# A gated mixture of experts after a depthwise convolution: the second part's first eight scatters as a group of their own, and an even two scatters a block

## The chip, the cores and the metric

The kernel runs on one core of a Trainium2 chip. The metric is the device time of one launch in microseconds (us), the median of several runs. A profile of one execution gives the time of each instruction on each engine: PE (matrix products), DVE (vector), ACT (activations and copies), POOL (here mainly the issuer of indirect DMAs) and SP (here the issuer of plain DMAs).

## The reference: what is computed

The input `x` has 8 sequences of 3584 tokens with 192 channels. A causal convolution with 7 softmaxed taps per head gives every token its row. Then each token goes to one of 8 experts: the expert with the highest logit where the token's local gate is below 0.5 (or at the start of a sequence), otherwise the expert of the token before it. The expert is a two-layer network, 192 to 1024 to 192.

```python
for b in range(B):
    prev_e = -1
    for s in range(S):
        fresh_e = int(np.argmax(logits[b, s]))
        if s == 0 or local_gate[b, s] < 0.5:
            e = fresh_e
        else:
            e = prev_e if prev_e >= 0 else fresh_e
        prev_e = e
        ...
        h = np.maximum(x[b, s] @ w1[e], 0.0)
        out[b, s] = p[e] * (h @ w2[e])
```

## The kernel before, in words

All products are in float32. The 28672 tokens are cut into 16 parts of 1792 tokens (`PT`). For each part the kernel does three things: it convolves (`conv`, for parts 0 and 1 a wider form on PE, `wide`), it routes (`route`, or `wide_route`: logits, expert, the token's place among the tokens of its expert), and it scatters the rows into `slots`, a table in DRAM with a stretch for each expert. A scatter (`put`, L762) is one indirect DMA from POOL: in part 0 and part 1 a part has 16 of them with 112 rows each, later 14 with 128 rows each. They wait in the list `to_put`, an entry of which is the group number, the rows and the places.

The expert networks run over **blocks** (L879 to L881): first 35 units of 128 tokens, then blocks of two units, then the rest. A unit is run as soon as it is surely full. `ONE` (L54) gives how many units are surely full after part g whatever the routing: 7 after part 0, 21 after part 1, 35 after part 2. So blocks 0 to 6 belong to group 0, blocks 7 to 20 to group 1, blocks 21 to 34 to group 2. `tables(g)` (L748) calls `table` (L782), 19 small DVE instructions that write the expert and the row of every unit of group g; part 0 has a form of its own, `first_table`.

A block does this, in order, in the loop at L1128:

- `ensure` (L1080) issues the row loads of the blocks up to three ahead on SP (`load_rows`, L901). The first load of a group waits for every scatter of that group to land (L909 to L913). A load is left for a later round if scatters of its group are still in `to_put`.
- `weights` issues the expert's weights of the block three ahead on SP (`load_w`, 1.5 MB, four buffers).
- `hidden` (L941) runs the first layer on PE (L952) and ACT (L957), and after each half issues as many scatters as `shares` says.
- `turn` (L922) transposes the rows of the next block on PE (L356) and copies them on ACT (L938).
- `output` (L962) runs the second layer on PE (L969) into two PSUM buffers `yps`. ACT scales one half into `o_sb` (L977, two buffers), DVE adds the other half (L981), and an indirect DMA from POOL sends the rows to the result (L985).
- `step` fills DVE with instructions of the next convolution and routing, by a budget of time per call; they stand in DVE's queue ahead of L981.

Each engine takes its instructions in the order written out by the program. SP's queue holds rows and weights mixed, so a row load that waits holds back the weights behind it. Indirect DMAs of `put` and of `output` go through one software queue.

In `wide_route` for part 1 (L390), the scatters are listed at L484 and L485, and then `place` and `base` (the tokens so far of every expert) and the tables follow at L489 to L493, all before the loop of blocks begins. The 16 scatters of part 1 are issued in blocks 1 to 4, four a block: `shares` is (1, 3) for blocks 1 to 4.

Of the kernel before, what the change touches and what calls it, by code (L numbers as in the profile page):

```python
# [9 lines left out]
I32 = mybir.dt.int32  # L10
Act = mybir.ActivationFunctionType
Alu = mybir.AluOpType
# [5 lines left out]
P = 128  # L18
# [5 lines left out]
UT = 128  # L24
NT = 14
PT = P * NT
NPART = N // PT
# [5 lines left out]
NH = NB // 2  # L33
# [14 lines left out]
def _sure(tokens, size):  # L48

    return max(0, -(-(tokens - E * (size - 1)) // size))  # L50
# [2 lines left out]

ONE = [_sure(min(g + 1, EARLY) * PT, UT) for g in range(NPART)]  # L54
TWO = [_sure((g + 1) * PT - ONE[-1] * UT, BT) if g >= EARLY else 0 for g in range(NPART)]
REST = NU - ONE[-1] - 2 * TWO[-1]
DG = 3 + D + DR
Y0 = 2
# [19 lines left out]
def kernel(  # L78
# [10 lines left out]
    nc = tc.nc  # L89
    cst = ctx.enter_context(tc.tile_pool(name="cst", bufs=1))  # L90
# [9 lines left out]
    op = ctx.enter_context(tc.tile_pool(name="op", bufs=2))  # L100
# [90 lines left out]
    def wide(g, xv, y_sb, both):  # L191
# [75 lines left out]
        for q in range(4):  # L267
# [8 lines left out]
                            base=0, pattern=[[1, P]], channel_multiplier=-1)  # L276
# [34 lines left out]
    eo = cst.tile([P, E], F32, name="eo")  # L311
# [25 lines left out]
    base = cst.tile([P, E], F32, name="base")  # L337
# [10 lines left out]
    tabi = {}  # L348

    def halves():  # L350
        return [(half, slice(half * DR, (half + 1) * DR)) for half in range(2)]
# [38 lines left out]
    def wide_route(g, y_sb, lt):  # L390

        y, tr = y_sb[:TB], ident[:TB, :TB]
# [63 lines left out]
        if g:  # L456
# [4 lines left out]
                                                op=Alu.is_equal)  # L461
# [9 lines left out]
        upto = sm.tile([P, E, 1 + NB], F32, name="upto")  # L471
# [9 lines left out]
        posi = sm.tile([P, NB], I32, name="posi", bufs=3)[:TB]  # L481
        nc.vector.tensor_copy(posi, pos)
        nc.vector.tensor_tensor(y[:, :, 0], pr, rs, op=Alu.mult)
        for b in range(NB):  # L484
            to_put.append((g, y[:, b, :], posi[:, b:b + 1]))  # L485
        yield
        if g == 0:
            first_table(upto[:, :, NB], pos)
        nc.vector.tensor_copy(place, upto[:, :, NB])  # L489
        nc.vector.tensor_tensor(base, place, eo, op=Alu.subtract)  # L490
        if g:
# [256 lines left out]
    def tables(g):  # L748
        if ONE[g] > (ONE[g - 1] if g else 0):
            yield from table(0, g, 1, ONE[g])  # L750
        if TWO[g] > (TWO[g - 1] if g else 0):
            yield from table(1, g, 2, TWO[g])
        if g == NPART - 1:
# [3 lines left out]
    to_put = []  # L757
    puts = []
# [23 lines left out]
    def table(kind, g, size, cap):  # L782


        end = ends[kind]
        new = sm.tile([P, E], F32, name="new")
        ni = sm.tile([P, E], I32, name="ni")
        nc.vector.scalar_tensor_tensor(new, used, -float(UT), base, Alu.mult, Alu.add)
        yield 0.2
        if cap is None:  # L790
            nc.vector.tensor_scalar(new, new, float(UT - 1), None, Alu.add)
            yield 0.2
        nc.vector.tensor_copy(ni, new)
        yield 0.2
        nc.vector.tensor_scalar(ni, ni, (UT * size).bit_length() - 1, None, Alu.arith_shift_right)
        yield 0.2
        nc.vector.tensor_copy(new, ni)
        yield 0.2
        nc.vector.tensor_copy(end[:, 0:1], end[:, E:])
        yield 0.2  # L800
        nc.vector.tensor_tensor_scan(end[:, 1:], new, new, end[:, 0:1], Alu.add, Alu.max)
        yield 0.2
        if cap is not None:
            nc.vector.tensor_scalar(end, end, float(cap), None, Alu.min)
            yield 0.2
        inn = sm.tile([P, E], F32, name="inn")
        nc.vector.tensor_scalar(inn, end[:, :E], i_of, None, Alu.is_le)
        yield 0.2
        nc.vector.scalar_tensor_tensor(inn, end[:, 1:], i_of, inn, Alu.is_gt, Alu.mult)
        yield 0.2  # L810

        row = sm.tile([P, E], F32, name="row")
        nc.vector.scalar_tensor_tensor(row, end[:, :E], -float(size), used, Alu.mult, Alu.add)
        yield 0.2
        nc.vector.tensor_tensor(row, row, eb, op=Alu.add)
        yield 0.2
        add = sm.tile([P, 3, E], F32, name="add")
        nc.vector.scalar_tensor_tensor(add[:, 0, :], row, pf[:, size - 1:size], inn,
                                       Alu.add, Alu.mult)
        yield 0.2  # L820
        nc.vector.tensor_tensor(add[:, 1, :], ef, inn, op=Alu.mult)
        yield 0.2
        nc.vector.tensor_copy(add[:, 2, :], inn)
        yield 0.2
        sums = sm.tile([P, 3], F32, name="sums")
        nc.vector.tensor_reduce(sums, add, axis=AX.X, op=Alu.add)
        yield 0.2
        nc.vector.tensor_tensor(tab[kind], tab[kind], sums, op=Alu.add)
        yield 0.2
        ti = cst.tile([P, 2], I32, name=f"tabi{kind}_{g}")  # L830
        if cap is None:

            no = sm.tile([P, 1], F32, name="no")
            nc.vector.tensor_scalar(no, tab[kind][:, 2:3], -float(DUMMY), float(DUMMY),
                                    Alu.mult, Alu.add)
            yield 0.2
            nc.vector.tensor_tensor(tab[kind][:, 0:1], tab[kind][:, 0:1], no, op=Alu.add)
            yield 0.2
        nc.vector.tensor_copy(ti, tab[kind][:, 0:2])
        yield 0.2  # L840
        tabi[kind, g] = ti
        nc.vector.tensor_tensor(new, end[:, 1:], end[:, :E], op=Alu.subtract)
        yield 0.2
        nc.vector.scalar_tensor_tensor(used, new, float(size), used, Alu.mult, Alu.add)
        yield 0.2
# [30 lines left out]
            to_put.append((g, pad, toi[:, e:e + 1]))  # L876


    blocks = [(0, 1, i, next(g for g in range(NPART) if i < ONE[g])) for i in range(ONE[-1])]  # L879
    blocks += [(1, 2, i, next(g for g in range(NPART) if i < TWO[g])) for i in range(TWO[-1])]  # L880
    blocks += [(2, 1, i, NPART - 1) for i in range(REST)]  # L881

# [18 lines left out]
    def load_rows(i):  # L901
        n, group = blocks[i][1], blocks[i][3]
        r = entry(i, 0, DUMMY + 1 - n)
        xg = xp.tile([P, KT, DG], F32, name="xg")
        get = nc.sync.dma_start(
            out=xg[:, :n, :].rearrange("p k d -> p (k d)"),
            in_=slots.rearrange("(r p) d -> r (p d)", p=UT)[bass.ds(r, n)]
            .rearrange("o (p x) -> (o p) x", x=n * DG))
        if group not in waited:  # L909
            waited.add(group)  # L910
            for g, ins in puts:
                if g == group:
                    tc.add_manual_dep(get.ins, ins.name, SYNC, reason="a row of the block")  # L913
        for g in range(group + 1, NPART):
            if any(p[0] == g for p in puts):
                tc.declare_no_dep(get.ins, group=f"puts{g}", reason="not in a unit full before")
        tc.add_to_no_dep_group("gets", get.ins)
        return xg
# [22 lines left out]
    def hidden(n, wb, xT, shares=(1, 1)):  # L941
        hT = hp.tile([P, FK, BT], F32, name="hT")
        w = slice(0, n * P)


        for two in range(2):
            hps = [hps_p.tile([P, 2, BT], F32, name="hps") for half in range(2)]
            for d in range(KD):
                for j in range(2):
                    f0 = (d * 4 + two * 2 + j) * P  # L950
                    for half, rows in halves():
                        nc.tensor.matmul(hps[half][:, j, w], lhsT=wb[rows, f0:f0 + P],  # L952
                                         rhs=xT[rows, d, w], start=(d == 0 and j == 0),
                                         stop=(d == KD - 1), skip_group_check=True)
            for half in range(2):
                m = half * 4 + two * 2
                relu = nc.scalar.activation(hT[:, m:m + 2, w], hps[half][:, :, w], Act.Relu)  # L957
            for _ in range(shares[two]):
                put(relu)
        return hT  # L960
# [117 lines left out]
    wbs, xgs = {}, {}  # L1078
# [40 lines left out]
    xT, _ = turn(blocks[0][1], xgs[0])  # L1119
# [8 lines left out]
    for i, (_, n, _, _) in enumerate(blocks):  # L1128
        st["block"] = i
        ensure(i)  # L1130
        weights(i + AHEAD)
        if i == LATE:
            x_in[3] = load_x(3)

        hT = hidden(n, wbs[i], xT, (0, 0) if i == 0 else (1, 3) if i < 5 else (1, 1))
        if i + 1 < len(blocks):
            xT, copied = turn(blocks[i + 1][1], xgs[i + 1])
            if len(to_put) > NT // 2 and n == KT:
                put(copied)
        step(2.1 if n == 1 else 4.2)  # L1140
        output(n, wbs.pop(i), xgs.pop(i), hT)
        step(1.3 if n == 1 else 3.0)

    kind, _, at, group = spare[0]
    any_left = nc.values_load(tabi[kind, group][at:at + 1, 0:1], min_val=0, max_val=DUMMY,  # L1145
                              skip_runtime_bounds_check_because="an entry of the table")
    with tc.If(any_left < DUMMY):
        for block in spare:
            blocks.append(block)
            i = len(blocks) - 1  # L1150
            n = block[1]
            xg = load_rows(i)
            wb = load_w(i)
            xT, _ = turn(n, xg)
# [68 lines left out]
```

## Time and profile before

| | |
|---|---|
| median of 3 runs | 1362.19 us (1357.04 to 1363.54) |
| span of the profiled execution | 1335.1 us |
| PE busy | 1314.4 us, 98% |
| DVE, ACT, POOL busy | 58%, 38%, 37% |
| DMA mean over the span | 255 GB/s |

The profiled execution is shorter than the timed ones, so times within the launch are read from the profile, and the forecast takes differences from it and puts them on the median. The profile's table of slices has PE at 98 or 99 per cent nearly everywhere but in the first four slices of 33 us, and the granted PE clock at full speed but for the third, which has 0.8 of it. The change lies in that stretch: blocks 0 to 20 run from about 45 us to 170 us. A timeline line has start, duration, engine and line, operation, tiles, count, and in brackets how long the engine was idle before it and for what.

### The profile page before, as it was taken

Reading aid. Unit: us, or ns where it says so; the run is one execution under the profiler, and the core shown is the slowest. Engines: PE = TensorE matmul, PEld = TensorE weight load, DVE = VectorE, ACT = ScalarE, POOL = GpSimd, SP = SyncE. Lnnn points to the kernel's source line nnn. Section 1 sums busy time; section 2 is a strip of 40 time slices with the busy share of each in tenths; the row PEclk is TensorE's granted clock in tenths of the full one; section 3 lists DMA queues with packets and bytes.
Section 4 is the critical chain, followed back from the end, with each engine's and each line's share of the span. In section 5 each row is a group of like instructions: output and inputs, shape, how many; then the busy total and the mean of one; then the engine's idle time right before and its main releaser. Section 6 shows DMA issues by size and latency. Waiting matters only on the chain. (4 is left out here: it accounts for less than half of the span.)

```text
span 1335.1 us, 41872 instructions
## 1 busy us (share of the span) xinstructions
PE 1314.4 (98%) x17140; PEld 1256.5 (94%) x17140; DVE 775.9 (58%) x2414; ACT 510.6 (38%) x1147; POOL 493.3 (37%) x538
## 2 busy tenths in 40 slices
PE   8889999999999999999999999999999999999998
PEld 7889999999999999999999999999999999999997
DVE  5969898977878787878787878785600000000000
ACT  5334444434343434343434343433333333333333
POOL 4544353534343434343434343434343211111111
PEclk9989999999999999999999999999999999999999
DMA  4899999966676767676767676756566555556993
GB/s 187 303 359 397 393 379 360 405 252 252 222 262 211 273 211 273 225 259 222 263 222 262 223 261 225 260 208 217 209 224 213 197 189 193 197 186 235 319 325 123
DMA packets 67299, 340.39 MB, mean 255 GB/s; under 512 B 12576, under 2 KB 23191, under 8 KB 47650
## 3 DMA queue, kind: packets, MB, share of 16 engines
q1 hardware_dynamic: 44784, 284.88, 59.0%
q0 software_dynamic: 22320, 52.82, 10.4%
q8 instruction: 136, 2.23, 0.6%
q14 instruction: 57, 0.47, 0.1%
q10 hardware_dynamic: 2, 0.00, 0.0%
HBM read 284.73 MB, written 53.41 MB: 253 GB/s over the span
## 5 line engine op out<-in xcount | busy, mean ns | idle before, releaser
L969 PE MATMUL yps<-wb,hT 64*128 64x192 f32 x7328 | 632.0, 325 | 0.2 <-issue 0.2
L952 PE MATMUL hps<-xT,wb 64*128 64x256 f32 (+1 forms) x6816 | 626.2, 336 | 4.7 <-ACT ls L579 3.0
L952 PEld LDWEIGHTS hps<-xT,wb 64*128 64x128 f32 x6816 | 563.4, 187 | 44.6 <-ACT ls L579 3.2
L969 PEld LDWEIGHTS yps<-wb,hT 64*128 64x128 f32 x7328 | 597.7, 188 | 2.8 <-issue 2.7
L985 POOL DMA_INDIRECT out_dram<-o_sb,xg x229 | 231.8, 1012 | 644.1 <-DVE o_sb L981 574.8
L957 ACT ACTIVATE hT<-hps 128x512 f32<-128x512 f32 (+1 forms) x568 | 261.3, 512 | 351.7 <-PE hps L952 351.7
L384 DVE SCALAR_TENSOR_TENSOR y_sb<-x_sb,c,y_sb 128x336 f32<-128x336 f32 x672 | 377.3, 571 | 18.1
L981 DVE SCALAR_TENSOR_TENSOR o_sb<-yps,xg,o_sb 128x192 f32<-128x192 f32 x229 | 87.4, 413 | 484.6 <-ACT o_sb L977 482.7
L769 POOL DMA_INDIRECT slots<-y_sb,posi x228 | 229.1, 1005 | 169.6 <-ACT hT L957 93.0
L977 ACT ACTIVATE o_sb<-yps,xg 128x192 f32<-128x192 f32 x229 | 86.9, 418 | 431.0 <-PE yps L969 417.7
L938 ACT COPY xT<-xps 128x768 f32<-128x768 f32 (+1 forms) x142 | 96.8, 682 | 7.3 <-PE xps L356 7.3
L356 PEld LDWEIGHTS xps<-ident,xg 64*128 64x128 f32 x1374 | 67.3, 139 | 11.8 <-DMA xg<-slots 2.4
L356 PE MATMUL xps<-ident,xg 64*128 64x64 f32 x1374 | 68.7, 222 | 3.5 <-DMA xg<-slots 3.5
L374 ACT ACTIVATE y_sb<-x_sb,c 128x336 f32<-128x336 f32 x112 | 64.6, 589 | 0.0
L564 DVE STREAM_TRANSPOSE z<-y_sb 128x768 f32<-128x768 f32 (+1 forms) x56 | 45.4, 853 | 0.4
L590 DVE COPY lt<-lq 32x36 f32<-32x36 f32 x224 | 40.9, 183 | 3.5
L574 PE MATMUL hps<-z,wg 64*32 64x128 f32 x1344 | 24.5, 273 | 1.3 <-issue 1.3
L574 PEld LDWEIGHTS hps<-z,wg 64*32 64x32 f32 x1344 | 20.0, 105 | 3.5 <-issue 2.0
L560 POOL COPY y_sb<-y_sb 128x896 f32<-128x896 f32 x14 | 13.3, 952 | 0.0
L548 PE MATMUL yps<-y_sb 112*128 112x194 f32 x64 | 11.5, 331 | 1.8 <-DVE y_sb L542 1.8
L548 PEld LDWEIGHTS yps<-y_sb 112*128 112x128 f32 x64 | 10.4, 189 | 2.6 <-DVE y_sb L542 2.0
L666 DVE COPY bk<-so_far 1x32 f32<-1x32 f32 x56 | 12.3, 220 | 0.7
(238 smaller groups left out, 366.9 us busy)
## 6 DMA issues: line engine op xcount, KB each, us to landing
wb<-in_w_dram SPq DMA_DIRECT2D x138, 1536.0 KB
x_sb<-in_x_dram SPq DMA_DIRECT2D x14, 1920.0 KB
xg<-slots SPq DMA_DIRECT2D x87, 259.0 KB
xg<-slots SPq DMA_DIRECT2D x53, 129.5 KB
wb<-in_w_dram SPq DMA_DIRECT2D x12, 512.0 KB
out_dram<-o_sb,xg POOLq DMA_INDIRECT x229
slots<-y_sb,posi POOLq DMA_INDIRECT x228
x_sb<-in_xb_dram SPq DMA_DIRECT2D x4, 768.0 KB
```

The lines of the kernel that those rows point to most:

```text
L356: nc.tensor.transpose(to, src[rows], identity=ident[rows, rows])
L374: nc.scalar.activation(cols(h), chans(h, 0), Act.Copy, scale=c[:, h, 0:1])
L384: nc.vector.scalar_tensor_tensor(cols(h), chans(h, k), c[:, h, k:k + 1], cols(h), Alu.mult, Alu.add)
L564: nc.vector.transpose(z[:, t:u, :], y_sb[:, t:u, Y0:Y0 + D])
L769: ins = nc.gpsimd.indirect_dma_start(out=slots[:, :], in_=rows, in_offset=None, out_offset=bass.IndirectOffsetOnAxis(ap=to, axis=0)).ins
L938: copied = nc.scalar.copy(to, at)
L952: nc.tensor.matmul(hps[half][:, j, w], lhsT=wb[rows, f0:f0 + P], rhs=xT[rows, d, w], start=(d == 0 and j == 0), stop=(d == KD - 1), skip_g ...
L957: relu = nc.scalar.activation(hT[:, m:m + 2, w], hps[half][:, :, w], Act.Relu)
L969: nc.tensor.matmul(yps[half][:, k * D:(k + 1) * D], lhsT=hT[rows, m, k * P:(k + 1) * P], rhs=wb[rows, WA + m * D:WA + (m + 1) * D], start= ...
L977: nc.scalar.activation(o_sb[:, k, :], y[k][0], Act.Copy, scale=xg[:, k, 0:1])
L981: nc.vector.scalar_tensor_tensor(o_sb[:, k, :], y[k][1], xg[:, k, 0:1], o_sb[:, k, :], Alu.mult, Alu.add)
L985: sent = nc.gpsimd.indirect_dma_start(out=out, in_=o_sb[:, k, :], in_offset=None, out_offset=bass.IndirectOffsetOnAxis(ap=xg.bitcast(I32)[ ...
```

## The change

Part 1 is split in two groups for scattering and for tables. `HALF` is 0.5, a group number between 0 and 1. `FULL` says how many units are surely full after each group: 7 after group 0, 14 after `HALF` (2688 tokens), 21 after group 1, and so on. The first eight scatters of part 1 (its first 896 tokens) carry the group `HALF`, and a table is written for this group, from the counts after eight of the sixteen chunks. Blocks 7 to 13 now belong to `HALF`, so their first row load waits for eight scatters and not for sixteen. Further, `shares` is (1, 1) from block 1 on: part 1 is scattered in blocks 1 to 8, two a block. The purpose is that block 7's rows no longer wait for all of part 1, and that scatters do not crowd in four blocks.

```diff
+HALF = 0.5
+FULL = {0: ONE[0], HALF: _sure(PT + PT // 2, UT), **{g: ONE[g] for g in range(1, NPART)}}
...
         for b in range(NB):
-            to_put.append((g, y[:, b, :], posi[:, b:b + 1]))
+            to_put.append((HALF if g and b < NH else g, y[:, b, :], posi[:, b:b + 1]))
         yield
         if g == 0:
             first_table(upto[:, :, NB], pos)
+        else:
+            nc.vector.tensor_tensor(base, upto[:, :, NH], eo, op=Alu.subtract)
+            for _ in table(0, HALF, 1, FULL[HALF]):
+                pass
...
-        ti = cst.tile([P, 2], I32, name=f"tabi{kind}_{g}")
+        ti = cst.tile([P, 2], I32, name=f"tabi{kind}_{int(2 * g)}")
...
-    blocks = [(0, 1, i, next(g for g in range(NPART) if i < ONE[g])) for i in range(ONE[-1])]
+    blocks = [(0, 1, i, next(g for g in FULL if i < FULL[g])) for i in range(ONE[-1])]
...
-        for g in range(group + 1, NPART):
-            if any(p[0] == g for p in puts):
+        for g in FULL:
+            if g > group and any(p[0] == g for p in puts):
                 tc.declare_no_dep(get.ins, group=f"puts{g}", reason="not in a unit full before")
...
-
-        hT = hidden(n, wbs[i], xT, (0, 0) if i == 0 else (1, 3) if i < 5 else (1, 1))
+        hT = hidden(n, wbs[i], xT, (1, 1) if i else (0, 0))
```

## The prediction

> **What bounds the kernel now.** I read the page first. PE is busy in almost all of the span:
>
> ```profile
> PE 1314.4 (98%) x17140; PEld 1256.5 (94%) x17140; DVE 775.9 (58%) x2414; ACT 510.6 (38%) x1147; POOL 493.3 (37%) x538
> ```
>
> So the change, which takes no work from PE, can only win back time in which PE stands still or runs at a lower clock. The view of waits of PE, from 0 to 300 us, says for what it stood still longest:
>
> ```profile
> PE xps L356 <- DMA xg<-slots: 3.5, 2, 2.1
> PE hps L952 <- ACT ls L579: 3.0, 1, 3.0
> ```
>
> Two waits for rows (3.5 us) and one for ACT (3.0 us). The timeline from 74 to 150 us shows where the larger ones lie, around blocks 6 and 7:
>
> ```profile
> 87.71 0.42 ACT L977 ACTIVATE o_sb<-yps,xg 128x192 f32<-128x192 f32 x1 [7.52 <-DMA out_dram<-o_sb,xg]
> ...
> 88.33 2.25 PE L952 MATMUL hps<-xT,wb 64*128 64x128 f32 x24 [3.00 <-ACT ls L579]
> ...
> 90.58 1.23 SPq L905 DMA_DIRECT2D xg<-slots  x2
> ...
> 92.68 0.58 PE L356 MATMUL xps<-ident,xg 64*128 64x64 f32 x6 [2.10 <-DMA xg<-slots]
> ...
> 93.06 4.41 PE L969 MATMUL yps<-wb,hT 64*128 64x192 f32 x32
> ...
> 97.31 2.84 PE L952 MATMUL hps<-xT,wb 64*128 64x128 f32 x48
> ```
>
> ACT stands 7.52 us in front of an `o_sb` buffer that an output scatter has not yet left; the copy that PE needs is behind it. Then SP issues block 7's rows at 90.58, when the last of the 16 scatters (issued at 82.17) has landed, and PE waits for these rows. After that the second layer takes 4.41 us, where it takes 2.82 at 100.17: the clock is down. The view of windows of 1 us (columns: length, busy PE, weight loads, DVE, ACT, POOL, clock, DMA share, GB/s):
>
> ```profile
> 89.00:90.00 1.00, 1.00 (x18) 1.00 (x16) 0.95 (x5) 0.01 (x1) 0.84 (x1) 0.73 0.18 60
> 90.00:91.00 1.00, 0.58 (x5) 0.29 (x2) 0.92 (x7) 0.70 (x2) 0.00 (x0) 0.50 0.29 98
> ...
> 96.00:97.00 1.00, 1.00 (x14) 1.00 (x14) 0.00 (x0) 0.00 (x0) 0.00 (x0) 0.86 0.99 397
> ```
>
> Half clock from about 89.5 to 96.3, 6.8 us. Price of this stall from block starts (first L952 of each): block 6 to 7 is 97.31 - 83.72 = 13.59 us, and an undisturbed block is 102.82 - 97.31 = 5.51, so 8.08 lost. Block 5 to 6, which also has logits, takes 83.72 - 75.96 = 7.76; the same pair of works later takes 148.56 - 141.43 = 7.13, so 0.63 lost. Together **8.7 us**.
>
> The last view is the timeline of 40 to 75 us, because the change puts DVE work there:
>
> ```profile
> 49.20 0.17 DVE L788 SCALAR_TENSOR_TENSOR new<-used,base 128x8 f32<-128x8 f32 x1
> ...
> 52.67 0.17 DVE L844 SCALAR_TENSOR_TENSOR used<-new,used 128x8 f32<-128x8 f32 x1
> 52.75 3.46 DVE L384 SCALAR_TENSOR_TENSOR y_sb<-x_sb,c,y_sb 128x336 f32<-128x336 f32 x6
> ...
> 56.13 0.41 DVE L981 SCALAR_TENSOR_TENSOR o_sb<-yps,xg,o_sb 128x192 f32<-128x192 f32 x1
> ...
> 56.55 0.40 PE L356 MATMUL xps<-ident,xg 64*128 64x64 f32 x6 [1.45 <-DMA xg<-slots]
> ...
> 56.76 2.85 PE L969 MATMUL yps<-wb,hT 64*128 64x192 f32 x32
> ```
>
> DVE has no gap here: part 1's table, six convolution steps, then block 0's L981, which ends at 56.54. Block 1's second layer starts at 56.76. It writes the PSUM buffer that L981 reads. That PE waited for rows at this moment hides that it could not have gone on much earlier for DVE either.
>
> [...] PE's clock is halved [...] 0.50 for 6.8 us, [...] after a gap of 3.0 us; a gap of 1.45 us (55.1 to 56.55) left it at 1.00. [...] ACT's ready copy at L579 sat behind L977. [...] part 0's last scatter ended on POOL at 52.50 and its waiter went at 54.34, 1.8 us. Under load the trace shows far more (below), so I take the trace. [...]
>
> **The change part by part.**
>
> *Two scatters a block.* POOL's work is the same (16 scatters near 1.0 us), off the path. What matters is the software queue. Before, five indirect DMAs a block (four scatters, one output) in 5.5 us, with DMA share near 1.0. Landings seen by their waiters: the output scatter issued at 70.35 frees `o_sb` for ACT at 78.30, the next (77.12) at 87.71. Five landings in 9.4 us, 1.9 us each: five a block need 9.4 us of a 5.5 us block, so the queue grows. After, three a block need 5.6: nearly balanced. The nearest row for three a block is this kernel's part 2, scattered two a block from 111 us on: its output scatters land about 6 to 7 us after POOL is done with them (104.43 + 0.97 to SP's next row load at 111.90; 110.19 + 0.97 to 118.25), with DMA share 1.0 and no PE or ACT wait. `o_sb` allows about 8.3 us (two blocks, 11.0, less 2.7 from L977 to the scatter's end). So the ACT stall goes, margin about 1.5 us.
>
> *Rows of blocks 7 to 13 wait for eight scatters.* The eighth is issued in block 4. With the PE times of the sum below (block 4 starts near 76) POOL is done with it near 81, landed by 83 to 88; block 7's rows are wanted near 91, and a load takes 2.1 us (90.58 to 92.68). It fits, with 1 to 6 us to spare. SP waits from about 77 to then and holds back weights of block 8, due near 99; before they were issued at 92.38 for 102.82, 10.4 us, without a wait. The second eight end in block 8, and block 14 is far. So the 8.7 us go whole. Part 2's scatters start in block 9 in both.
>
> *One more table.* One subtraction and 19 instructions on DVE. Part 1's table took 49.20 to 52.75 = 3.55 us, the subtraction 0.2: **3.75 us**. A second instance of the table (110.10 to 113.81) gives 3.71, so 3.7 to 3.9. Queued behind it: six convolution steps, L981 of block 0, then its output scatter on POOL and part 1's first scatters. Waiting for L981: PE. L981 ends at 60.3 and not 56.54, block 1's second layer starts near 60.45 and not 56.76: **3.7 us** lost. Nothing gives it back: PE does 5.51 us a block and DVE nine steps and L981, 5.5 us.
>
> *Clock.* PE then idles from 55.1 to 60.45 but for 0.4 us of transposes. [...] I take **1.6**.
>
> *Group numbers, names, no-dependence declarations.* No instruction: nothing.
>
> Sum: -8.7 + 3.7 + 1.6 = **-3.4 us**, 1362.19 - 3.4 = 1358.8.
>
> **The rivals.** *A: no new stall*, DVE's delay being absorbed, because PE waits at 56.55 for rows anyway. For it: PE's named wait there is rows. Against: L981 ended only 0.2 us before. Time 1362.2 - 8.7 = 1353.5. *B: the old stall stays and the new one is added*: the queue is near balance at three a block, and x's load of part 3 falls in this stretch; a late eighth scatter would hold SP again. Then +5.3 with none of the 8.7 won: 1367.5, slower. Against: part 2's stretch ran with three a block. *C: timed runs lose more here than the profile.* They are 25 us longer than the profiled one, and nothing in it says where. If the DMA-saturated first stage is slower in them, the scatter stall is larger too; at twice 8.7, less 5.3, the time is 1350.1. Against: 25 us may be a constant around the launch.
>
> **How the numbers follow.** Forecast 0.50, A 0.20, C 0.15, B 0.15. Within 0.5% means 1355.4 to 1369.0. Medians of three scatter by some 3 us (1357.04 to 1363.54). Faster: most of A (0.15), nearly all of C (0.14), a tail of the forecast (0.08): 0.37. Slower: a good half of B (0.08) and tails (0.03): 0.11. Same: 0.52. Range 1350 to 1367.5, from C's time to B's.
>
> **What would show it.** Right: block 6 to 7 in about 5.5 us, no ACT wait for the output scatter, block 7's rows issued before 88; and PE idle until about 60.4 before block 1's second layer, with L981 of block 0 ending at 60.3, and clock below 1 soon after. Wrong: L981 early or PE not waiting for it (A); SP's row load of block 7 after 90, ACT's wait at L977 still there (B).

## The result and the profile after

| | before | after | ratio (95% interval) |
|---|---|---|---|
| time of the launch, us | 1360.84 (1357.04 to 1363.54, 4 runs) | 1351.43 (1349.61 to 1353.02, 4 runs) | 0.9932 (0.9904 to 0.9961) |

The change takes 9.4 us, 0.68%. The forecast was 3.4 us and, as the likeliest class, "within 0.5%" (0.52, against 0.37 for faster). The median so missed that class, and the interval of the gain reaches from 0.39% to 0.96%. The measured time lies in the range, but near its lower end, at rival C's value; that it lies there is luck, since the range goes so far down only for C, and what C describes did not come (below).

One thing has to be known to read any number below: each series of runs shows the kernel before either at about 1336 us or at about 1357 to 1361 us; the result above and the first three series of experiments are at the **long level**, while the profile of before that the prediction was drawn from (1335.1 us) and the last series are at the **short level**.

So the profile after is to be read against two profiles of before: the one of the prediction (short level) and one of the same kernel at the long level (`r1_before` below). The page of after, busy times of the engines:

```profile
PE 1327.7 (98%) x17140; PEld 1298.5 (96%) x17140; DVE 780.0 (58%) x2434; ACT 512.1 (38%) x1147; POOL 492.6 (36%) x538
```

DVE has the 20 instructions more that the new table costs (2434 against 2414) and 4.1 us more work. The engines' own work is otherwise the same. PE is "busy" for 13 us more than in the shorter profile of before, with the same 17140 matmuls: it is not the amount of work that differs between the levels.

The waits of PE from 44 to 110 us in after:

```profile
PE yps L977 <- ACT hT L965: 4.2, 4, 2.9
PE hps L960 <- issue: 0.4, 2, 0.3
```

The wait for block 7's rows (2.1 us) and the wait for ACT's copy of the logits (3.0 us) are gone, as forecast; so is the other wait for rows, block 1's 1.4 us, which was to stay. The wait for DVE's L989 (L981 before), which the forecast put in their place, is not there. What PE waits for is ACT's L965, the relu of the first layer; each half of the first layer ends in a pair of relus on ACT, and the second layer begins with what the pairs have made. The timeline of after from 54 to 72 us shows why:

```profile
55.00 0.66 ACT L965 ACTIVATE hT<-hps 128x256 f32<-128x256 f32 x2 [4.92 <-remote]
...
55.43 2.93 PE L977 MATMUL yps<-wb,hT 64*128 64x192 f32 x16 [2.91 <-ACT hT L965]
...
58.15 4.52 PE L960 MATMUL hps<-xT,wb 64*128 64x128 f32 x48
...
61.14 0.41 DVE L989 SCALAR_TENSOR_TENSOR o_sb<-yps,xg,o_sb 128x192 f32<-128x192 f32 x1
...
62.69 2.82 PE L977 MATMUL yps<-wb,hT 64*128 64x192 f32 x32
...
68.59 0.27 PE L960 MATMUL hps<-xT,wb 64*128 64x128 f32 x1
...
68.89 0.95 POOL L777 DMA_INDIRECT slots<-y_sb,posi  x1 [0.30 <-issue]
...
70.36 0.66 ACT L965 ACTIVATE hT<-hps 128x256 f32<-128x256 f32 x2 [2.26 <-PE xps L360]
70.79 1.28 PEld L977 LDWEIGHTS yps<-wb,hT 64*128 64x128 f32 x16 [0.69 <-ACT hT L965]
```

Two things are to be seen. Block 0's second pair of relus comes at 55.00, after ACT was idle for 4.92 us, so PE is already late. It then runs at half clock (granted 0.50 from 55 to 61 us), block 1's first layer takes 4.52 us (2.84 at the full clock in the prediction's timeline, 97.31), and its second layer starts at 62.69, after L989 has ended (61.55): DVE's table is hidden. And the last matmul of block 2's first layer ends by 68.86, but its relu starts only at 70.36, with ACT idle for 2.26 us. Between them lies a scatter's issue on POOL, 68.89 to 69.84. ACT starts 0.52 us after its end. No buffer and no data of the scatter is wanted by the relu.

Block 7's rows are issued at 90.86 (90.58 in the prediction's profile), in the timeline of SP in after from 66 to 105 us:

```profile
90.86 1.25 SPq L913 DMA_DIRECT2D xg<-slots  x2
```

Still, PE does not wait for them, since it comes to block 7 later here.

Where the time went is read from the start of a block, its first relu on ACT. All in us:

| stretch | before, short | changed, short (`r12`) | before, long (`r1`) | after, long |
|---|---|---|---|---|
| start of block 1 | 53.67 | 53.46 | 60.34 | 61.02 |
| block 1 to 7 | 45.24 | 43.07 | 46.50 | 38.42 |
| block 7 to 35 | 163.61 | 161.86 | 172.58 | 175.26 |
| block 35 to 118 | 915.53 | 915.21 | 923.67 | 918.85 |
| block 118 to the end | 157.05 | 157.19 | 157.6 | 157.66 |
| span | 1335.1 | 1330.8 | 1360.7 | 1351.2 |

At the long level the change gives 8.1 us in blocks 1 to 6, loses 2.7 in 7 to 34, and gives 4.8 where the program is the same in both. Of the 2.7 lost, 1.9 are in blocks 7 and 8, which now have two scatters each (6.35 and 6.57 us, 5.52 in `r1_before`). The 4.8 all lie in the ten blocks of two units with logits: 133.4 us in `r1_before`, 128.6 in after, while the other 73 blocks of that stretch take 790.3 in both. At the short level the change gives 2.2 and 1.8 in the first two stretches, and nothing to speak of after. The windows of the first stretch, at the long level, `r1_before` (columns: length, busy PE with its instructions, weight loads, DVE, ACT, POOL, clock, DMA share, GB/s):

```profile
60.00:106.80 46.80, 41.84 (x619) 38.69 (x617) 28.34 (x70) 16.11 (x44) 21.68 (x23) 0.95 0.90 333
```

and in after:

```profile
61.00:99.40 38.40, 37.43 (x615) 35.35 (x615) 29.55 (x72) 16.23 (x44) 19.21 (x19) 0.99 0.93 347
```

Nearly the same groups of matmuls (619 and 615) take 41.84 us of busy time before and 37.43 after, and PE's gaps fall from 4.96 to 0.97 us. POOL issues 23 times in the one and 19 times in the other, so in this stretch each scatter less goes with some two microseconds less (8.4 / 4). DMA's share is no higher in the slower stretch.

### The profile page after: what moved, and what is told of

Same layout as the page of the kernel before. It is cut to its first block, busy times and chain, and to the rows that moved or that the text cites. A ratio compares the mean times of both kernels' runs of the same rounds, so it can differ in the third digit from the quotient of the medians.

```text
span 1351.2 us, 41902 instructions
## 1 busy us (share of the span) xinstructions
PE 1327.7 (98%) x17140; PEld 1298.5 (96%) x17140; DVE 780.0 (58%) x2434; ACT 512.1 (38%) x1147; POOL 492.6 (36%) x538
## 3 DMA queue, kind: packets, MB, share of 16 engines
q0 software_dynamic: 22320, 52.82, 10.3%
## 5 line engine op out<-in xcount | busy, mean ns | idle before, releaser
L977 PE MATMUL yps<-wb,hT 64*128 64x192 f32 x7328 | 652.9, 326 | 9.6 <-ACT hT L965 7.7
L960 PE MATMUL hps<-xT,wb 64*128 64x256 f32 (+1 forms) x6816 | 640.2, 337 | 0.6 <-issue 0.6
L977 PEld LDWEIGHTS yps<-wb,hT 64*128 64x128 f32 x7328 | 609.7, 188 | 21.0 <-ACT hT L965 14.0
L960 PEld LDWEIGHTS hps<-xT,wb 64*128 64x128 f32 x6816 | 610.0, 188 | 8.4 <-issue 1.8
L965 ACT ACTIVATE hT<-hps 128x512 f32<-128x512 f32 (+1 forms) x568 | 262.3, 512 | 407.5 <-PE hps L960 306.8
L989 DVE SCALAR_TENSOR_TENSOR o_sb<-yps,xg,o_sb 128x192 f32<-128x192 f32 x229 | 87.4, 413 | 489.1 <-ACT o_sb L985 474.5
L985 ACT ACTIVATE o_sb<-yps,xg 128x192 f32<-128x192 f32 x229 | 86.9, 418 | 379.1 <-PE yps L977 368.7
L360 PEld LDWEIGHTS xps<-ident,xg 64*128 64x128 f32 x1374 | 81.9, 139 | 2.7
L360 PE MATMUL xps<-ident,xg 64*128 64x64 f32 x1374 | 80.4, 222 | 0.0
L556 PE MATMUL yps<-y_sb 112*128 112x194 f32 x64 | 12.5, 351 | 1.8 <-DVE y_sb L550 1.6
L590 DVE STREAM_TRANSPOSE lq<-ls 128x256 f32<-128x256 f32 x14 | 6.2, 444 | 12.4 <-ACT ls L587 12.4
L568 POOL COPY y_sb<-y_sb 128x896 f32<-128x896 f32 x14 | 13.4, 954 | 0.0
```

What stands on the lines that cost most here:

```text
L360: nc.tensor.transpose(to, src[rows], identity=ident[rows, rows])
L977: nc.tensor.matmul(yps[half][:, k * D:(k + 1) * D], lhsT=hT[rows, m, k * P:(k + 1) * P], rhs=wb[rows, WA + m * D:WA + (m + 1) * D], start= ...
L985: nc.scalar.activation(o_sb[:, k, :], y[k][0], Act.Copy, scale=xg[:, k, 0:1])
L989: nc.vector.scalar_tensor_tensor(o_sb[:, k, :], y[k][1], xg[:, k, 0:1], o_sb[:, k, :], Alu.mult, Alu.add)
```

## The experiments

Every kernel here computes the whole reference. Ratios are to runs of before in the same series. Runs 1 to 4, 5 to 8, 9 to 11 and 12 are a series each, and each series ran on another chip.

**Run 1: before once more, with a profile.** No edit. The question was where the 25 us between the profile and the timed runs lie.

> The kernel before, unchanged, as a second profile of it. The forecast's reading: it looks as the first profile did, blocks of 5.51 us outside the stall, the 8.7 us stall at blocks 5 to 7, and a span near 1337. Rival C (timed runs lose more than the first profile shows): a span near 1358, with the extra 20 us in the profile as blocks of about 6.07 us, where ACT starts the second pair of L957 some 1.4 us late, as the changed kernel's profile has in many of its blocks; then the stall at blocks 5 to 7 is no smaller than 8.7 us.

Measured: 1362.42 us, beside a median of 1361.12 (25 runs), so now the long level has a profile. From 66 to 88 us in the timeline of `r1_before`:

```profile
69.16 2.81 PE L969 MATMUL yps<-wb,hT 64*128 64x192 f32 x31
...
71.25 0.94 POOL L769 DMA_INDIRECT slots<-y_sb,posi  x1 [0.31 <-issue]
...
72.88 0.53 PE L952 MATMUL hps<-xT,wb 64*128 64x128 f32 x5 [0.23 <-issue]
...
73.61 0.52 PE L952 MATMUL hps<-xT,wb 64*128 64x128 f32 x5 [0.21 <-issue]
...
74.00 0.94 POOL L769 DMA_INDIRECT slots<-y_sb,posi  x1 [0.30 <-issue]
...
75.81 1.62 PE L952 MATMUL hps<-xT,wb 64*128 64x128 f32 x24 [0.45 <-issue]
75.86 0.42 ACT L977 ACTIVATE o_sb<-yps,xg 128x192 f32<-128x192 f32 x1 [4.64 <-PE hps L952]
75.90 0.33 SPq L898 DMA_DIRECT2D wb<-in_w_dram  x1
```

The second layer of block 1 ends at 71.97, but ACT's copy L977, which needs nothing else by this view, starts at 75.86, when the four scatters are over (the last ends at 74.94), with 4.64 us idle. SP's weight load starts 0.04 us after it. PE's first layer goes in bursts of four or five matmuls with gaps named "issue". The stall of 7.52 us for the output scatter, the main item of the prediction, does not exist in this execution. Blocks 1 to 4, with four scatters each, take 7.94, 8.37, 8.04 and 8.58 us from first relu to first relu, where block 6, without scatters, takes 5.52: here the loss is spread over every block that scatters four times. In after, with two scatters, the same four take 6.42, 6.35, 6.09 and 6.06. Crowded scatters so cost more apiece: over 5.52 us, four a block cost 2.4 to 3.1 us, two a block 0.5 to 0.9, and up to 1.1 in block 8.

**Run 2: the table alone.** Before, with the subtraction and `table` for `HALF` in `wide_route`. Blocks, groups of the scatters and shares are as before.

```diff
+        else:
+            nc.vector.tensor_tensor(base, upto[:, :, NH], eo, op=Alu.subtract)
+            for _ in table(0, HALF, 1, FULL[HALF]):
+                pass
```

> The kernel before with the extra table and its subtraction alone; groups, row waits and shares as before. The forecast: block 0's addition on DVE ends 3.75 us later, block 1's second layer starts 3.7 us later[...]; slower than before by about 5.3 us (0.4%). Rival A (DVE's delay is absorbed): no difference.

Measured: 1364.05 us, ratio 1.0024 (1.0014 to 1.0035). The table costs 0.24%, some 3 us, where the scatters are crowded. The forecast said 5.3 us, by PE's wait for L989. That wait is not there: PE's list names none, and block 1's second layer starts at 60.53, while L989 ends at 60.78. So the forecast's path is not the one by which the table costs here; which one it is stays unshown.

**Run 3: the whole change but for the even shares.**

```diff
-        hT = hidden(n, wbs[i], xT, (1, 1) if i else (0, 0))
+        hT = hidden(n, wbs[i], xT, (0, 0) if i == 0 else (1, 3) if i < 5 else (1, 1))
```

> The changed kernel with the old shares: the group of eight stays, but sixteen scatters go in blocks 1 to 4. The forecast: the software queue is behind as before, ACT waits about 7 us for an output scatter near block 5 and PE loses 3 us and some clock; block 7's rows are issued early, since they wait for scatters of block 2, so the 2.1 us wait for rows goes; with the new stall's 5.3 us, slower than before by 1 to 4 us. If the row wait alone is what cost, the time is that of the changed kernel, 9 us under before.

Measured: 1363.58 us, ratio 1.0023 (1.0010 to 1.0037). The group of its own does what it is for, block 7's rows are issued at 81.11 instead of 95.67 in `r1_before`, and it gains nothing over run 2. So at this level the wait for rows was not what cost. With even shares the same kernel takes 1351.4: **the even shares alone are worth 1.0023 - 0.9932 = 0.91%, some 12 us** (0.6 to 1.2% by the two intervals, which come from two series). The two profiles differ by 10.3 us: run 3 starts block 1 3.5 us sooner, takes 12.0 more from block 1 to 7 (50.42 and 38.42), 1.2 less from 7 to 35, and 3.1 more after that. PE's waits from 44 to 70 us in run 3, and PE's timeline from 54 to 67 us:

```profile
PE yps L977 <- ACT hT L965: 2.8, 1, 2.8
PE yps L977 <- DVE o_sb L989: 1.5, 1, 1.5
```

```profile
55.88 2.85 PE L960 MATMUL hps<-xT,wb 64*128 64x128 f32 x48
...
58.74 0.54 PE L977 MATMUL yps<-wb,hT 64*128 64x192 f32 x2
60.75 2.70 PE L977 MATMUL yps<-wb,hT 64*128 64x192 f32 x29 [1.47 <-DVE o_sb L989]
```

Here the forecast stall on DVE does show, with 1.5 us. PE has waited 2.8 us for the relus, as in after (2.9), but is not slowed this time: block 1's first layer takes 2.85 us and not 4.52, so PE comes to the second layer at 58.74, ahead of L989. In after it is the half clock that hides DVE.

**Run 4: four output buffers.** Before, with `o_sb` as four tiles of one unit each.

```diff
-    op = ctx.enter_context(tc.tile_pool(name="op", bufs=2))
+    op = ctx.enter_context(tc.tile_pool(name="op", bufs=4))
...
-        o_sb = op.tile([P, KT, D], F32, name="o_sb")
+        o_sb = [op.tile([P, D], F32, name="o_sb") for k in range(n)]
```

> The kernel before with o_sb cut in tiles of one unit, four of them in the same memory, so that ACT may run four single units ahead of the output scatters and not two. Scatters and row waits as before. The forecast: the 7.52 us wait of ACT and PE's 3.0 us gap at block 6 go; the wait for block 7's rows stays until 90.5 and PE then stands about 5 us in one piece there, since it gets there 3 to 4 us sooner; so 0 to 3 us gained. If the ACT wait is the whole of the stall: 8 us gained.

Measured: 1360.07 us, ratio 0.9996 (0.9987 to 1.0005). ACT's wait for `o_sb`, the head of the stall in the prediction, costs nothing that shows at the long level.

After these four the theory was a new one: while POOL issues a scatter, starts on other engines are held, so what matters is *when* a scatter is issued. If so, the second pair of relus, which comes about 1.3 us after the first, is held by a scatter issued between the two pairs. Runs 5 and 6 move the scatters within a block, at the same number.

**Run 5: both scatters after the second pair of relus.**

```diff
-        hT = hidden(n, wbs[i], xT, (1, 1) if i else (0, 0))
+        hT = hidden(n, wbs[i], xT, (0, 2) if i else (0, 0))
```

> The changed kernel with shares (0, 2): the same two scatters a block, but both behind the second pair of L957 and none behind the first. New theory S, from the second profile of before and the changed kernel's: while POOL issues a scatter, and for about 0.55 us after, ACT and SP do not get going on what PE has finished; the scatter behind the first pair so makes the second pair late by 1.4 us and the block 0.55 us longer (6.07 for 5.51). S expects the blocks with scatters to take 5.51 again: some 20 blocks of single units, 8 to 12 us under the changed kernel, about 1341. The rival, that the scatters' DMA traffic is what slows these blocks, expects no difference, since the traffic is the same.

**Run 6: both after the first pair.**

```diff
-        hT = hidden(n, wbs[i], xT, (1, 1) if i else (0, 0))
+        hT = hidden(n, wbs[i], xT, (2, 0) if i else (0, 0))
```

> The changed kernel with shares (2, 0): both scatters behind the first pair of L957. Theory S: the second pair of L957 waits for both scatters, some 2.6 us late and not 1.4, and the block takes about 7.3 us; over some 20 to 25 blocks 25 to 30 us more than the changed kernel, about 1378. DMA traffic as the cause: no difference.

Measured: run 5 1366.79 us, ratio 1.0048 (1.0030 to 1.0065); run 6 1374.73 us, 1.0103 (1.0089 to 1.0118). From 118 to 131 us in the timeline of run 5:

```profile
124.32 0.66 ACT L965 ACTIVATE hT<-hps 128x256 f32<-128x256 f32 x2 [0.75 <-PE hps L960]
...
125.26 0.97 POOL L777 DMA_INDIRECT slots<-y_sb,posi  x1 [1.33 <-ACT hT L965]
126.53 0.96 POOL L777 DMA_INDIRECT slots<-y_sb,posi  x1 [0.30 <-issue]
126.68 2.88 PEld L960 LDWEIGHTS hps<-xT,wb 64*128 64x128 f32 x48
```

and the same place in run 6, from 127 to 134 us:

```profile
128.85 0.66 ACT L965 ACTIVATE hT<-hps 128x256 f32<-128x256 f32 x2 [0.50 <-PE hps L960]
129.97 0.96 POOL L777 DMA_INDIRECT slots<-y_sb,posi  x1 [0.30 <-issue]
131.24 0.96 POOL L777 DMA_INDIRECT slots<-y_sb,posi  x1 [0.30 <-issue]
132.16 0.66 ACT L965 ACTIVATE hT<-hps 128x256 f32<-128x256 f32 x2 [2.65 <-remote]
```

In run 6 the second pair comes 2.65 us after ACT went idle, in run 5 on time. Over blocks 0 to 34 the median delay of the second pair, from the end of PE's first layer to ACT's start, is 1.38 us in after, 0.1 in run 5, and 0.03 in both profiles of the short level. In run 6 it is some 2.0 us in twelve of these blocks, and mostly far less in the others. A block of one unit with two scatters mostly takes 6.0 to 6.1 us in after, 6.7 to 6.8 in run 6 and 5.4 to 5.6 in many blocks of run 5. The traffic is the same in all three, so it is not what sets these times. This part of the theory holds. The total of run 5 does not follow it: from block 35 to 118 it loses 18.8 us against after (937.63 and 918.85). There, blocks of two units with logits take 14.5 to 15.2 us, where after has 12.5 to 13.4. That the late scatters there are the reason is shown by run 9 below.

**Run 7: no convolution steps ahead of block 0's L989**, to take the new work off DVE where the forecast saw its stall.

```diff
-        step(2.1 if n == 1 else 4.2)
-        output(n, wbs.pop(i), xgs.pop(i), hT)
+        if i:
+            step(2.1 if n == 1 else 4.2)
+        output(n, wbs.pop(i), xgs.pop(i), hT, 1.2 if i else 0)
```

(`output` hands its last argument to its own `step`.)

> The changed kernel without the six convolution steps ahead of block 0's addition on DVE (they come later), which takes 3.5 us off DVE's queue there. The forecast: block 1's second layer starts 3.5 us sooner and the half clock goes: about 5 us under the changed kernel. Theory S: PE's second pair of block 0 is late for the scatters of part 0 anyway and half clock follows from that; PE has no gap for DVE's addition in the changed kernel's profile: no difference within 2 us.

**Run 8: runs 5 and 7 together.**

> Both of the edits of shares (0, 2) and of the light first block. Theory S: as shares (0, 2) alone, about 1341, within 2 us. The forecast's step on DVE: 5 us under shares (0, 2) alone.

Measured: run 7 1356.1 us, ratio 0.9964 (0.9951 to 0.9976); run 8 1366.92 us, 1.0042 (1.0027 to 1.0056). Run 8 is as run 5, and run 7, whose interval overlaps the plain change's, is not better than that. L989 of block 0 starts at 58.83 instead of 61.14 us, and block 1's second layer at 62.57 instead of 62.69: 2.3 us off DVE bring PE 0.1. DVE is off the path here, which agrees with after's list of waits. Block 5 starts 1.0 us sooner than in after. This lead is then lost at block 7, in the timeline of run 7 from 84 to 103 us:

```profile
89.82 1.25 SPq L913 DMA_DIRECT2D xg<-slots  x2
...
93.67 0.40 PE L360 MATMUL xps<-ident,xg 64*128 64x64 f32 x6 [2.00 <-DMA xg<-slots]
```

The rows come when the eight scatters have landed, 1.0 us sooner than in after; PE comes sooner still and waits 2.00 us. PE is slower after that wait: the second layer at 97.32 takes 3.66 us for 32 matmuls, where the one at 86.17 takes 2.82. Blocks 5 and 6 together take 17.5 us, where after has 13.5.

**Runs 9 to 11: late scatters where they helped, even ones where they did not.** Run 9 has (0, 2) in blocks of one unit and (1, 1) in blocks of two; run 10 adds run 7's edit; run 11 adds three scatters in blocks 1 and 2.

```diff
-        hT = hidden(n, wbs[i], xT, (1, 1) if i else (0, 0))
+        hT = hidden(n, wbs[i], xT, (0, 0) if i == 0 else (0, 2) if n == 1 else (1, 1))
```

> The changed kernel with shares (0, 2) in blocks of one unit and (1, 1) in blocks of two. With shares (0, 2) everywhere the first 35 blocks were 3.6 us sooner than in the changed kernel, and the blocks of two with logits lost 2 to 2.6 us each. Theory S: the gain of the first stage stays and the loss goes: 3 to 5 us under the changed kernel, 1347. If the traffic and not its place made the blocks longer, no difference from the changed kernel.

> The same, with the light first block. From the profile of both edits before (block 35 at 269.5 us against 271.1 without the light block, with a stall of 6 us in block 7, whose rows landed late): 0 to 3 us under the last, 1345; the stall in block 7 stays.

```diff
+        hT = hidden(n, wbs[i], xT, (0, 0) if i == 0 else (0, 3) if i < 3 else (0, 2) if n == 1 else (1, 1))
```

> The same again with three scatters behind the second pair in blocks 1 and 2, so that the eighth scatter goes out in block 3 and not in block 4. If block 7 waits for its eight scatters alone, its rows are loaded some 5 us sooner and its stall goes: 4 to 6 us under the last, 1340. If three a block crowd as four did, blocks 1 to 3 take 7 to 8 us and it is slower than the last by 2 to 5 us.

Measured, beside a before of 1357.49 us: run 9 1352.59, ratio 0.9961 (0.9948 to 0.9974); run 10 1348.12, 0.9926 (0.9905 to 0.9947); run 11 1348.72, 0.9941 (0.9920 to 0.9962). Expected were 1347, 1345 and 1340. None of them can be told from the plain change (0.9932, 0.9904 to 0.9961). Run 10 is 4.5 us below run 9, just clear of their intervals, so here the light first block seems to have helped; the two profiles (spans 1350.8 and 1350.6) do not show where. With (1, 1) again in blocks of two, the blocks with logits are back at 12.5 to 13.4 us. The second pair of relus is on time in all three (median delay at most 0.2 us), and yet block 7 to 35 takes 172.5 us in run 9 against 175.3. The timeline of run 9 from 84 to 97 us shows one place to which the loss moved:

```profile
88.13 0.85 PE L582 MATMUL hps<-z,wg 64*32 64x128 f32 x39
88.43 0.94 POOL L777 DMA_INDIRECT slots<-y_sb,posi  x1 [0.30 <-issue]
...
89.24 0.41 PE L582 MATMUL hps<-z,wg 64*32 64x128 f32 x3 [0.26 <-issue]
...
89.97 0.44 PE L582 MATMUL hps<-z,wg 64*32 64x128 f32 x4 [0.32 <-issue]
...
91.45 1.55 PE L582 MATMUL hps<-z,wg 64*32 64x128 f32 x49 [0.46 <-issue]
```

The logits' matmuls go in bursts of three and four, with gaps of 0.26 and 0.32 us, until POOL has issued all that stands behind 88.43. What is not taken from ACT is taken from PE's own instructions. So the edit of the shares moves the holding more than it removes it.

**Run 12: the change once more**, unaltered, in a series of its own.

> The changed kernel, unchanged, as a second profile of it. The gain as read from the first profiles: 9 to 10 us under before; about half of it by block 35, the other half in the blocks of two (864 us from block 40 to block 118, where the kernels with four scatters a block early took 867 to 869). If the second half was chance of one execution, those blocks take 867 or more here and the total is 1354 or more. Theory S: ACT's second pair of L957 again starts 0.5 to 0.6 us after a scatter's end. The forecast's step on DVE: PE waits for L989 of block 0 before block 1's second layer; the first profile has no such wait.

Measured: 1332.91 us (1330.67 to 1334.95, 17 runs) beside a before of 1335.62 (1333.11 to 1341.03, 21 runs), ratio 0.9978 (0.9971 to 0.9985). This series is at the short level, the prediction's own, with 2.7 us of gain. PE's waits from 44 to 110 us:

```profile
PE yps L977 <- DVE o_sb L989: 3.0, 1, 3.0
PE xps L360 <- DMA xg<-slots: 1.4, 1, 1.4
```

The stall on DVE that the forecast named heads the list. The 1.4 us for rows are block 1's, which the prediction's timeline had with 1.45. Its timeline from 53 to 72 us:

```profile
56.05 0.17 DVE L852 SCALAR_TENSOR_TENSOR used<-new,used 128x8 f32<-128x8 f32 x1
56.13 3.47 DVE L388 SCALAR_TENSOR_TENSOR y_sb<-x_sb,c,y_sb 128x336 f32<-128x336 f32 x6
...
59.51 0.41 DVE L989 SCALAR_TENSOR_TENSOR o_sb<-yps,xg,o_sb 128x192 f32<-128x192 f32 x1
...
59.98 5.17 PE L977 MATMUL yps<-wb,hT 64*128 64x192 f32 x29 [2.96 <-DVE o_sb L989]
...
67.54 0.95 POOL L777 DMA_INDIRECT slots<-y_sb,posi  x1 [0.30 <-ACT hT L965]
...
67.88 0.66 ACT L965 ACTIVATE hT<-hps 128x256 f32<-128x256 f32 x2 [0.62 <-PE hps L960]
```

Table, six convolution steps, L989, PE: the queue of the prediction, 0.4 us earlier. Then, at 67.88, the second pair of relus starts in the middle of a scatter's issue (67.54 to 68.49). This is the line to hold against 68.89 and 70.36 in after: same program, same place, nothing held. And the windows of 1 us:

```profile
58.00:59.00 1.00, 0.00 (x0) 0.00 (x0) 0.99 (x2) 0.00 (x0) 0.00 (x0) 0.66 0.94 377
60.00:61.00 1.00, 1.00 (x6) 1.00 (x8) 0.96 (x2) 0.00 (x0) 0.80 (x1) 0.50 1.03 397
...
65.00:66.00 1.00, 1.00 (x21) 1.00 (x19) 0.64 (x3) 0.77 (x2) 0.00 (x0) 0.93 0.98 406
```

PE stands still with DVE busy, then works at half clock (6 matmuls in a microsecond, then 21) until about 65.1.

## Why the prediction was right and wrong

**At the level of its own profile, it was right in nearly every step** (run 12 against the profile of before):

- *The old stall goes whole, 8.7 us.* Blocks 4 to 6 give 1.06 + 1.84 + 5.06 = 7.96 us, later blocks a little more (1.75 from 7 to 35). ACT's wait for `o_sb` is gone, PE's wait for block 7's rows too. Whether the even shares or the group of eight removed it no run at this level shows. These rows are issued at 88.51, "before 88" was said, and PE still does not wait.
- *A new stall of 3.7 us on DVE.* L981 was to end at 60.3 and PE to go on at 60.45. L989 ends at 59.92, PE goes on at 59.98, after 2.96 us idle.
- *Half clock, 1.6 us.* Its length was the author's estimate; no trace had shown it. 29 matmuls take 5.17 us; at the full clock, from 32 in 2.82 (after, 62.69), 2.56. So 2.6 us, 1.0 more than taken. Block 1 to 2 as a whole takes 13.14 us against 7.34: 5.80 lost, 5.3 forecast.
- *Sum.* -3.4 forecast; -4.3 in the spans of the two profiles and -2.7 in the timed runs.

**At the level of the timed median, the sum failed**: -9.4 us and not -3.4. The step that failed is the new stall with its clock, +5.3 us, and with it the assumption under which a profile's differences were put on the median. In after PE never waits for L989, and 2.3 us less on DVE bring PE 0.1 us (run 7). The reason lies in block 0: in `r1_before` and in after alike its second relus come late, after 4.80 and 4.92 us in which ACT was idle. PE waits 2.8 and 2.9 us for them and is slow after that (48 matmuls in 4.49 and 4.52 us), and when it comes to block 1's second layer, at 61.99 and 62.69, DVE is done (58.60 and 61.55). Where those 48 take 2.85 us (run 3), 1.5 us of the stall show.

The other term, -8.7 us, came out near its size, by another path. Blocks 1 to 6 give 8.1 us, but not by one stall that goes: four blocks of some 8.2 us become four of some 6.2. "POOL's work is the same, off the path" was wrong there: ACT, PE and SP start late while POOL issues (in `r1_before` ACT's copy after 4.64 us of idleness, PE with gaps of 0.21 to 0.45 us, SP's load 0.04 us after ACT), and crowded issues cost more than spread ones (2.4 to 3.1 us a block with four, 0.5 to 1.1 with two). Run 4 shows that the buffer wait at the root of the 8.7 is no cause at this level, and run 3 that the wait for rows is none. At the short level blocks 1 to 6 give 2.2 us with 5.8 lost to the new stall, so without it they would give 8.0, as at the long level. The stall is what sets the two levels apart in this stretch; the 4.8 us after block 35 come on top.

**The rivals.** C said that timed runs lose more than the profile and that the scatter stall is what grows in them: 1350.1 against 1351.4. The number is close by luck. Blocks 1 to 6 take only 1.3 us more in `r1_before` than in the short profile, the stall of the prediction is not in them, and DMA's share is about the same (0.90 and 0.88). C's premise was right in that the 25 us lie within the program; the argument held against it, that they may be a constant around the launch, was wrong: block starts put 6.7 us ahead of block 1, 1.3 in 1 to 6, 9.0 in 7 to 34, 8.1 in 35 to 117 and 0.5 after. A ("no new stall", 1353.5) is right at the long level and wrong at the short one, though not for its reason, PE's wait for rows. B's stall did not come in the change itself, but its worry about block 7 was sound: in runs 7, 8 and 10, in which PE comes earlier, it waits 2.0, 1.7 and 0.9 us for these rows.

**What stays open.** Of the gain at the long level, 4.8 us lie after block 35, in the ten blocks with logits, where the program is the same. Those take 13.3 us each in `r1_before` and 12.5 to 13.4 in after. Even shares do not settle it: run 7 has them and takes 131.5 us in the ten, about as much as runs 2 to 4 (131.8 to 132.4) and not after's 128.6, and its ratio is 0.9964. So for about half of the gain between the two profiles no cause is shown. Nor is it shown how POOL's issue holds the others. The relus start 0.5 to 0.6 us after a single scatter's end, time after time, but after several in a row it is 0.9 to 1.1 us (74.94 to 75.86 in `r1_before`), in run 6 the second pair starts just before the second scatter has ended (132.16 and 132.20), and not every instruction is held (in run 5 ACT's L985 starts in the middle of a scatter at 121.71). The packets of queue q8, which the page gives the kind "instruction", take 0.97 us in the median in the prediction's profile and in after, so longer packets there are not it. And what makes a series long or short is open: each of the four series had a chip of its own, and within none of them did the level change, so the chip cannot be told from the moment.

## What to carry to other kernels

Before differences from a profile are put on a median, hold the profile's span against it: 25 us of 1360 that no view explains may be a different balance of the engines, and then both the gain and the cost of a change have another size. Where starts on other engines follow the end of indirect DMAs' issue on POOL, as ACT's relus did here by 0.5 to 0.6 us, spread these over many blocks; here it was worth some 12 us at the long level, where more output buffers were worth nothing (run 4, 0.9996). A stall taken away brings at most the slack to the next wait: run 7 brought PE to block 5 1.0 us sooner and then lost 4.0 at block 7's rows. And a cost on another engine is paid only if the critical engine comes there first: the stall behind the table, clock and all, took 5.8 us at the short level and none in after, where PE was late.

## What the runs showed of the hardware that was not expected

- One program has two levels of time, 1336 and 1360 us, each steady within a series (spreads of 8 us in 21 runs and 7 us in 25). At the long one, ACT mostly starts the second pair of relus 0.5 to 0.6 us after a scatter's issue has ended on POOL, with a median delay of 1.38 us in after and 1.09 in `r1_before`; at the short one the delay is 0.03 us.
- Where in a block two scatters are issued moves the whole launch at the long level by 1.7% (0.9932 with one after each pair of relus, 1.0048 with both late, 1.0103 with both early).
- The row load that waits for the eighth scatter of 112 rows starts 6.2 us after that one's issue has ended in run 7 (89.82 and 83.65) and 7.5 us in run 12 (88.51 and 80.98; DMA's share 1.02 from 60 to 80 us).
- After the same gap of PE, 2.8 us, the 48 matmuls of block 1's first layer took 4.49 us in `r1_before` and 2.85 in run 3.
